# A new instruction order for a linear-attention kernel with a gated scan behind it

## The chip, the cores and the metric

The kernel runs on one core of one Trainium2 chip. The metric is the device time in microseconds (us). Times come from several executions, each with its own span (first to last instruction of the profile) and its own mean granted clock of TensorE. Below, a *hole* is a stretch in which TensorE stands idle, and a *fall* is a drop of its granted clock to half.

## The reference, cut to what matters

```python
# attention part; q, k, v: 8 batches, 8 heads, 576 tokens, 64 wide
q_s = np.exp(q - np.max(q, axis=-1, keepdims=True))
q_s = q_s / (np.sum(q_s, axis=-1, keepdims=True) + 1e-09)
...                                    # k_s: the same over the tokens (axis 2)
kv = np.einsum('bhsd,bhse->bhde', k_s, v)
return np.einsum('bhsd,bhde->bhse', q_s, kv).astype(np.float32)

# gated scan part; x: the heads put side by side, 576 x 512 per batch
proj = x @ w_in
val, gate = (proj[..., :D_inner].copy(), proj[..., D_inner:].copy())
a = np.exp(A_log)[None, None, :]
...
for t in range(S):
    h = a[0, 0] * h + val[:, t, :]
    ys[:, t, :] = h
silu = gate * (1.0 / (1.0 + np.exp(-gate)))
return (silu * ys @ w_out).astype(np.float32)
```

(The first two lines join several of the original.)

## The kernel before: the parts that matter

The whole kernel is driven by one string, ORDER. Each entry emits the instructions of one step, and every engine executes its own instructions strictly in the order of this string. `norm/P.3.0` is the normalization of the first half of batch 3 on POOL (GpSimd); `/A` is ACT (ScalarE), `/D` is DVE (VectorE). Entries without a letter have a fixed engine. Tokens are cut in 9 chunks of 512 for the projections (`val`, `gate`), scans and outputs, and in 8 batches of 576 for the attention part.

```python
def decay(self, e, m):                       # one row of scan factors; e is the engine of the fill
    copy(e, decay[:, m], acol[:, m:m + 1].broadcast_to([128, 2 * W]))
    nc.gpsimd.memset(decay[:, m, W:W + 1], 0.0)     # the column where a batch begins: always GpSimd

def norm(self, e, b, q2):                    # eq *= 1 / row sum
    ...
def transp(self, e, b, g):                   # six 128 x 128 transposes of eq on TensorE
    ...
def kv(self, e, b, q2):                      # k^T v, 36 matmuls of 64 x 65
    ...
def xa(self, e, b, q2):                      # x^T, columns 0..503 of the batch
def xr(self, e, b):                          # x^T, the remaining 72 columns
def _proj(self, dst, i, col):                # four matmuls of 128 x 512 (val or gate)
    ...
RINGS = {..., "qf": 2, "kf": 2, "vf": 2, "tp": 1, "ax": 1, "pp": 3, "po": 2, ...}   # buffers
```

The detail on which this case turns is the second line of `decay`: an entry `decay/A.2` puts a long copy (1.04 us) into ACT's order and a tiny clearing (0.10 us) into GpSimd's order. The clearing has to wait for the copy.

The softmax here doesn't subtract the row's maximum and nothing guards it: scores larger than these inputs give would overflow.

## Time and profile before

| what | kernel before |
|---|---|
| time, median of 3 | 145.68 us |
| span of the profiled execution | 142.5 us (time 144.23 us), clock 1.000 |
| TensorE, VectorE, ScalarE, GpSimd busy | 119.6, 114.6, 98.9, 92.2 us |
| first projection starts | 22.89 us |
| first projection of chunk 1 starts | 37.99 us |
| last matmul ends | 138.46 us |

The lines of the profile are shown in the prediction below. Until about 38 us loads, softmax and casts set the pace; from there TensorE is practically never idle (busy 99.58 of the 100.47 us up to its last matmul). A time line entry reads: start, duration (both us), engine, source line, operation, output <- inputs, shapes, count, and in brackets how long the engine stood idle just before and whose end released it. The letter x with a number is the count of merged instructions.

```profile
26.63 0.10 POOL L232 MEMSET decay<- 128x1 f32 x1 [2.33 <-ACT decay L192]
26.75 2.12 POOL L263 TENSOR_TENSOR eq<-eq,qs 128x1152 bf16<-128x1152 bf16 x1
```

Here GpSimd stands 2.33 us at a clearing of one column, with the normalization of batch 2 behind it.

### The profile page before, as it was taken

What the parts mean: (1) busy time and instruction counts of PE and PEld (TensorE: products, weight loads), DVE (VectorE), ACT (ScalarE), POOL (GpSimd) and SP (SyncE); (2) the same over time, 40 slices, a digit from 0 to 9 for tenths busy, and PEclk for the clock granted to TensorE, in tenths of its full rate; (3) what the DMA queues carried; (4) which work ended last, traced back from release to release, by engine and by line L of the source; (5) the groups of instructions that cost most, each with busy time, mean ns of one, the idle gap of its engine ahead of it and who ended that gap; (6) DMA issues with size and microseconds to landing.
All of it is one profiled execution on the core that took longest, in us unless ns stands there. A gap on an engine that the chain in (4) does not pass through costs nothing.

```text
span 142.5 us, 3185 instructions
## 1 busy us (share of the span) xinstructions
PE 119.6 (84%) x1269; PEld 61.7 (43%) x1284; DVE 114.6 (80%) x146; ACT 98.9 (69%) x138; POOL 92.2 (65%) x80
## 2 busy tenths in 40 slices
PE   0024586987599999999999999999999999999980
...
DVE  0358669879998898989998889999789798989630
...
DMA  4999999999999999999999999999543433007195
GB/s 111 401 399 391 391 390 389 391 393 391 389 389 392 391 391 391 387 404 403 394 325 382 399 240 208 263 408 392 110 83 121 181 147 147 0 0 289 71 343 190
DMA packets 24243, 42.29 MB, mean 297 GB/s; under 512 B 5666, under 2 KB 5922, under 8 KB 24227
## 3 DMA queue, kind: packets, MB, share of 16 engines
...
HBM read 31.46 MB, written 9.44 MB: 287 GB/s over the span
## 4 chain that ended last, share of the span: by engine, by line
PE 70%; DMA 14%; DVE 5%; POOL 3%; issue 3%; SPq 2%; ACT 0%; POOLq 0%; ACTq 0%; DVEq 0%
PE pp L377 38%; PE po L423 21%; DMA kf<-in_k_dram 7%; DMA y<-in_moe_w_in_dram 6%; PE ax L290 4%; PE tp L271 3%; POOL eq L263 3%; SPq L188 2%; DVE qs L255 2%; PE pp L333 1%; PE ax L333 1%; DVE u L404 1%; DVE xT L194 1%; PE pp L423 1%; PE pp L360 1%
## 5 line engine op out<-in xcount | busy, mean ns | idle before, releaser
L377 PE MATMUL pp<-xT,win 128*128 128x512 bf16 (+1 forms) x308 | 68.0, 363 | 1.9 <-ACT xT L192 1.2
L408 POOL TENSOR_TENSOR z<-u,y 128x512 bf16<-128x512 f32 x29 | 37.3, 1297 | 24.2 <-DVE u L404 15.6
L377 PEld LDWEIGHTS <-win 128*128 128x128 bf16 x320 | 30.6, 99 | 31.5 <-issue 4.4
L396 DVE TENSOR_TENSOR_SCAN y<-decay,y,pp 128x512 f32<-128x512 f32 x32 | 39.6, 1262 | 1.4 <-PE pp L377 1.3
L263 POOL TENSOR_TENSOR eq<-eq,qs 128x1152 bf16<-128x1152 bf16 x16 | 33.8, 2119 | 7.9 <-DVE qs L258 7.7
L423 PE MATMUL po<-wout,z 128*128 128x512 bf16 x134 | 33.7, 379 | 0.3
L401 ACT ACTIVATE th<-pp 128x512 f32<-128x512 f32 x36 | 21.5, 597 | 15.8 <-PE pp L377 15.6
L404 DVE SCALAR_TENSOR_TENSOR u<-th,pp 128x512 f32<-128x512 f32 x36 | 24.4, 683 | 5.3 <-ACT th L401 4.8
L255 DVE TENSOR_REDUCE qs<-eq 128x36 f32<-128x2304 bf16 (+1 forms) x10 | 20.6, 2057 | 6.6 <-ACT eq L235 6.6
L271 PE MATMUL tp<-ident,eq 128*128 128x128 bf16 x108 | 10.9, 249 | 13.3 <-POOL eq L263 11.8
L235 ACT ACTIVATE eq<-qf 128x1152 bf16<-128x1152 f32 x16 | 18.3, 1158 | 5.3 <-DMA qf<-in_q_dram 5.3
L430 ACT ACTIVATE ob<-po 128x512 f32<-128x512 f32 x28 | 16.6, 599 | 7.6 <-PE po L423 7.6
L423 PEld LDWEIGHTS <-z 128*128 128x128 bf16 x148 | 13.9, 98 | 15.3 <-issue 1.0
L241 ACT ACTIVATE ek<-kf 128x2304 bf16<-128x2304 f32 (+1 forms) x10 | 17.2, 1736 | 0.5 <-DMA kf<-in_k_dram 0.5
L194 POOL CAST vb<-vf 128x1152 bf16<-128x1152 f32 (+1 forms) x14 | 14.9, 1080 | 3.7 <-DMA vf<-in_v_dram 3.6
L271 PEld LDWEIGHTS <-eq 128*128 128x128 bf16 x108 | 8.3, 111 | 17.4 <-POOL eq L263 13.2
L192 ACT ACTIVATE xT<-pp 128x504 bf16<-128x504 f32 (+1 forms) x20 | 7.8, 443 | 4.4 <-PE pp L333 2.6
L290 PE MATMUL ax<-vb,ek 64*64 64x65 bf16 x576 | 7.3, 199 | 1.5 <-ACT ek L241 1.1
L290 PEld LDWEIGHTS <-ek 64*64 64x64 bf16 x576 | 6.2, 112 | 4.7 <-issue 2.2
L192 ACT ACTIVATE eqT<-tp 128x768 bf16<-128x768 bf16 x8 | 6.5, 810 | 1.6 <-PE tp L271 1.6
L192 ACT ACTIVATE xT<-ax 128x1008 bf16<-128x1008 f32 x7 | 7.1, 1016 | 0.3 <-PE pp L360 0.3
L432 DVE TENSOR_SCALAR ob<-po 128x512 f32<-128x512 f32 x6 | 4.1, 684 | 3.2 <-PE po L423 3.2
...
## 6 DMA issues: line engine op xcount, KB each, us to landing
...
```

The lines of the kernel that those rows point to most:

```text
L192: nc.scalar.activation(out, in_, AF.Copy)
L235: nc.scalar.activation(buf("eq", b)[:, q2].rearrange("p c h d -> p h c d"), buf("qf", b)[:, 2 * q2:2 * q2 + 2].rearrange("p h (c d) -> p h ...
L255: nc.vector.tensor_reduce(s[:, 0, n].rearrange("p (a o) -> p a o", o=1), buf("eq", b)[:, h].rearrange("p q c h d -> p (q c h) d"), axis=AX ...
L263: eng[e].tensor_tensor(x, x, r.rearrange("p (a o) -> p a o", o=1) .broadcast_to([128, 2 * C, D]), ALU.mult)
L271: nc.tensor.transpose(tp[:, j, :], src[:, 6 * g + j, :], ident)
L290: nc.tensor.matmul(kvp[o:o + 64, h2, q2 * E1:(q2 + 1) * E1], lhsT=ek[r, 2 * q2 + hp2, c * D:(c + 1) * D], rhs=vb[r, 2 * q2 + hp2, c, :], s ...
L377: nc.tensor.matmul(dst[:, a:z], lhsT=win[:, kt, col:col + 128], rhs=xT[:, kt, s0:s0 + z - a], start=(kt == 0), stop=(kt == 3))
L396: nc.vector.tensor_tensor_scan(buf("y", (i, m)), a, buf("pp", ("v", i, m)), init, op0=ALU.mult, op1=ALU.add)
L401: nc.scalar.activation(buf("th", (i, m)), buf("pp", ("g", i, m)), AF.Tanh, scale=0.5)
L404: nc.vector.scalar_tensor_tensor(buf("u", (i, m)), buf("th", (i, m)), 1.0, buf("pp", ("g", i, m)), op0=ALU.add, op1=ALU.mult)
L408: eng[e].tensor_tensor(buf("z", i)[:, m], buf("u", (i, m)), buf("y", (i, m)), ALU.mult)
L423: nc.tensor.matmul(self._po(i, r, h), lhsT=buf("z", i)[:, m, r * 128:(r + 1) * 128], rhs=wout[:, m, self._cols(h)], start=(m == 0), stop=( ...
```

## The change

The intent: a new order of instructions and loads for all engines, in which TensorE finds work earlier. The two strings hold the same 556 entries; some of them change engine. The load of A_log goes from SP's queue to ACT's. New forms of the transposes and of the projections are added as methods, but no entry of the new order uses them. Cut to its core:

```diff
-lq.0.1 expq.0.1 lq.0.0 lq.1.- qsum.0.1 expq.0.0 norm/P.0.1 qsum.0.0 transp.0.2 expq.1.0 lk.0.0
-...
-val.1.0 vcast/P.2.0 tanh.1.2 gmul.1.2 vcast/P.2.1 val.1.3 expk.2.- norm/P.3.0 gate.1.1 scan.1.0
-transp.3.0 val.1.2 tanh.1.1 tevac/A.3.0 scan.1.3 norm/P.3.1 kv.2.0 cwout/A.0 gmul.1.1 scan.1.2
-...
+lalog lq.0.1 lq.0.0 lq.1.- expq.0.1 qsum.0.1 lk.0.1 lv.0.0 expq.0.0 norm/P.0.1 expq.1.0 expk.0.1
+...
+xbevac/D.1.1 cwout/A.1 tevac/A.2.2 gate.1.2 gate.1.0 qsum.3.- tanh.1.2 tanh.1.0 expk.2.-
+zmul/P.0.2 decay/P.0 val.1.0 outp.0.3 decay/A.2 gmul.1.2 outp.0.2 gmul.1.0 lq.4.- oevac/A.0.3
+oevac/A.0.2 norm/P.3.0 val.1.2 scan.1.0 transp.3.0 vcast/P.2.1 gate.1.3 gate.1.1 tanh.1.3 lk.3.-
+...
-            nc.sync.dma_start(out=alog, in_=moe_A_log.rearrange("(o n) -> o n", o=1))
+            nc.scalar.dma_start(out=alog, in_=moe_A_log.rearrange("(o n) -> o n", o=1))
+        def transp4(self, e, b, g):        # not called by the new order
+        ...
-        def _proj(self, dst, i, col):
+        def _proj(self, dst, i, col, q2=None):      # q2 is always None in the new order
```

The scan factors are filled in another order and on other engines, too: before `decay/A.3 decay/P.2 decay/A.0 decay/P.1`, now `decay/A.1 decay/P.3 decay/P.0 decay/A.2`.

More of the change, by code (lines that the diff above doesn't have):

```diff
@@ L23 @@
 ORDER = """
-lq.0.1 expq.0.1 lq.0.0 lq.1.- qsum.0.1 expq.0.0 norm/P.0.1 qsum.0.0 transp.0.2 expq.1.0 lk.0.0
-tevac/A.0.2 lv.0.1 norm/P.0.0 transp.0.0 lk.0.1 expk.0.0 expq.1.1 qsum.1.0 tevac/D.0.0
-vcast1/P.0.2 lalog lv.0.0 expk.0.1 norm/P.1.0 vcast1/D.0.3 vcast1/P.0.0 qsum.1.1 vcast1/A.0.1
-transp.0.1 tevac/D.0.1 lq.2.- kv.0.1 lwin.0.0 lwin.2.0 lwin.3.0 kv.0.0 transp.1.0 tevac/A.1.0
-lwin.1.0 lwin.1.1 norm/P.1.1 kvn.0 lwin.0.1 xt.0.0.1 xt.0.1.1 cwin/P.2.0 expq.2.0 xevac/D.0.0.1
-transp.1.1 xt.0.0.0 tevac/D.1.1 xevac/A.0.1.1 transp.1.2 xt.0.1.0 xevac/D.0.0.0 lwin.2.1
@@ L30 @@
-cwin/D.0.0 cwin/P.1.0 cwin/P.3.0 lwin.3.1 cwin/P.1.1 xevac/D.0.1.0 expq.2.1 talog val.0.3 acol
-tevac/A.1.2 lk.1.- cwin/A.2.1 cwin/P.0.1 val.0.1 lv.1.- cwin/A.3.1 gate.0.0 decay/A.3 qsum.2.-
-scan.0.3 gate.0.3 tanh.0.0 scan.0.1 norm/P.2.0 decay/P.2 gmul.0.0 norm/P.2.1 tanh.0.3 vcast/P.1.1
-gmul.0.3 expk.1.1 transp.2.0 val.0.0 expk.1.0 lq.3.- scan.0.0 gate.0.2 val.0.2 tanh.0.2
-tevac/D.2.0 vcast/A.1.0 gate.0.1 zmul/P.0.3 transp.2.1 kv.1.1 gmul.0.2 scan.0.2 kv.1.0 lv.2.-
-tanh.0.1 lk.2.- lwout.0 kvn.1 lwout.1 gmul.0.1 lq.4.- xr.1 xrevac/D.1 xa.1.0 decay/A.0
@@ L36 @@
-tevac/D.2.1 expq.3.0 expq.3.1 lk.3.- xa.1.1 xbevac/A.1.1 zmul/P.0.0 xaevac/A.1.0 transp.2.2
-tevac/A.2.2 xbevac/D.1.0 gate.1.3 tanh.1.3 zmul/P.0.1 zmul/P.0.2 gate.1.2 qsum.3.- gmul.1.3
-val.1.0 vcast/P.2.0 tanh.1.2 gmul.1.2 vcast/P.2.1 val.1.3 expk.2.- norm/P.3.0 gate.1.1 scan.1.0
-transp.3.0 val.1.2 tanh.1.1 tevac/A.3.0 scan.1.3 norm/P.3.1 kv.2.0 cwout/A.0 gmul.1.1 scan.1.2
-gate.1.0 tanh.1.0 kv.2.1 expq.4.0 transp.3.1 cwout/P.1 kvn.2 expq.4.1 outp.0.2 tevac/D.3.1 xr.2
-decay/P.1 xa.2.0 transp.3.2 zmul/P.1.2 xrevac/D.2 gmul.1.0 outp.0.3 lv.3.- xa.2.1 qsum.4.-
@@ L42 @@
-val.1.1 lq.5.- zmul/P.1.0 zmul/P.1.3 oevac/A.0.2 xaevac/A.2.0 lv.4.- lk.5.- oevac/A.0.3
-vcast/P.3.1 xbevac/A.2.0 vcast/P.3.0 xbevac/A.2.1 scan.1.1 tevac/D.3.2 outp.0.0 outp.0.1 expk.3.-
-val.2.2 gate.2.1 scan.2.2 tanh.2.1 oevac/A.0.0 val.2.1 lk.4.- gmul.2.1 kv.3.1 kv.3.0 gate.2.0
-oevac/A.0.1 gate.2.2 expq.5.1 tanh.2.0 store.0.1 norm/P.4.0 zmul/P.1.1 scan.2.1 kvn.3 gmul.2.0
-tanh.2.2 val.2.3 transp.4.0 expq.5.0 norm/P.4.1 gmul.2.2 scan.2.3 outp.1.0 xa.3.0 xr.3 outp.1.1
-zmul/P.2.2 tevac/A.4.0 xrevac/A.3 lq.6.- qsum.5.- oevac/A.1.0 xa.3.1 xbevac/A.3.0 lv.5.-
@@ L48 @@
-xbevac/A.3.1 vcast/P.4.0 vcast/P.4.1 zmul/P.2.1 gate.2.3 outp.1.3 transp.4.1 tanh.2.3 val.2.0
-tevac/D.4.1 norm/P.5.1 gmul.2.3 scan.2.0 xaevac/A.3.0 zmul/P.2.3 transp.4.2 oevac/A.1.1 val.3.1
-val.3.3 expk.4.- scan.3.1 scan.3.3 tevac/D.4.2 norm/P.5.0 expk.5.- oevac/A.1.3 val.3.0 kv.4.1
-kv.4.0 gate.3.0 tanh.3.0 zmul/P.2.0 scan.3.0 outp.1.2 val.3.2 vcast/P.5.0 gate.3.2 gmul.3.0
-vcast/P.5.1 expq.6.0 oevac/A.1.2 tanh.3.2 expq.6.1 scan.3.2 kvn.4 transp.5.0 gate.3.1 outp.2.3
-gmul.3.2 tevac/D.5.0 xa.4.0 store.0.0 zmul/P.3.2 store.1.0 xr.4 zmul/P.3.0 tanh.3.1 xaevac/A.4.0
@@ L54 @@
-outp.2.0 gmul.3.1 xrevac/A.4 transp.5.1 oevac/A.2.3 kv.5.1 kv.5.0 store.1.1 lk.6.- xa.4.1
-gate.3.3 xbevac/A.4.1 qsum.6.- kvn.5 xbevac/A.4.0 outp.2.2 val.4.1 tanh.3.3 tevac/A.5.1
-oevac/A.2.0 gate.4.2 zmul/P.3.1 norm/P.6.0 gmul.3.3 tanh.4.2 transp.5.2 val.4.2 scan.4.1 gmul.4.2
-zmul/P.3.3 gate.4.0 tevac/A.5.2 gate.4.1 oevac/A.2.2 tanh.4.0 outp.3.1 scan.4.2 lv.6.- lq.7.-
-gmul.4.0 dtransp.6.0 vcast/P.6.0 xa.5.0 xa.5.1 tanh.4.1 gmul.4.1 store.2.1 oevac/D.3.1
-xbevac/D.5.1 norm/P.6.1 vcast/P.6.1 outp.2.1 expk.6.- val.4.0 xaevac/A.5.0 xbevac/D.5.0 outp.3.0
@@ L60 @@
-scan.4.0 kv.6.0 xr.5 zmul/P.4.2 dtransp.6.1 kv.6.1 val.4.3 xrevac/A.5 gate.5.1 zmul/D.4.1
-expq.7.1 gate.4.3 oevac/D.2.1 oevac/A.3.0 scan.4.3 zmul/P.4.0 tanh.5.1 tanh.4.3 kvn.6 expq.7.0
-outp.3.2 val.5.1 lv.7.- gmul.5.1 gmul.4.3 val.5.2 outp.3.3 scan.5.1 zmul/P.4.3 oevac/A.3.2 xa.6.1
-scan.5.2 zmul/P.5.1 outp.4.2 xbevac/A.6.0 store.2.0 store.3.0 qsum.7.- xbevac/A.6.1 xr.6
-vcast/P.7.0 oevac/A.3.3 xa.6.0 val.5.0 xrevac/A.6 outp.4.0 vcast/A.7.1 norm/P.7.1 val.5.3
-scan.5.0 oevac/A.4.2 xaevac/A.6.0 gate.5.3 scan.5.3 lk.7.- store.3.1 tanh.5.3 gate.5.2 tanh.5.2
@@ L66 @@
-outp.4.3 gmul.5.3 gate.6.0 gate.5.0 oevac/D.4.0 gmul.5.2 tanh.6.0 gmul.6.0 zmul/P.5.3 tanh.5.0
-val.6.2 gmul.5.0 val.6.3 outp.4.1 expk.7.- scan.6.2 gate.6.2 kv.7.1 kv.7.0 gate.6.3 oevac/A.4.1
-tanh.6.2 scan.6.3 dtransp.7.1 norm/P.7.0 gmul.6.2 kvn.7 zmul/D.5.2 val.6.1 dtransp.7.0 tanh.6.3
-oevac/A.4.3 zmul/P.5.0 val.6.0 gmul.6.3 outp.5.3 scan.6.1 scan.6.0 outp.5.2 zmul/D.6.2
-oevac/A.5.3 xr.7 xa.7.0 store.4.1 outp.5.1 xrevac/A.7 store.4.0 xa.7.1 xaevac/A.7.0 xbevac/D.7.0
-gate.6.1 xbevac/A.7.1 oevac/D.5.2 gate.7.0 val.7.0 zmul/P.6.0 tanh.6.1 tanh.7.0 gmul.6.1 gmul.7.0
@@ L72 @@
-outp.5.0 val.7.2 oevac/D.5.1 zmul/P.6.3 gate.7.2 scan.7.0 zmul/P.6.1 scan.7.2 outp.6.3 store.5.1
-val.7.3 oevac/A.5.0 gate.7.1 tanh.7.2 gmul.7.2 scan.7.3 tanh.7.1 gmul.7.1 gate.7.3 tanh.7.3
-val.8.2 val.7.1 gmul.7.3 zmul/P.7.0 val.8.0 outp.6.1 oevac/A.6.3 outp.6.0 scan.8.2 gate.8.1
-scan.7.1 scan.8.0 gate.8.2 zmul/D.7.3 oevac/A.6.1 tanh.8.1 gmul.8.1 gate.8.0 zmul/D.7.2
-zmul/D.7.1 oevac/A.6.0 tanh.8.2 outp.6.2 gmul.8.2 tanh.8.0 store.5.0 val.8.1 outp.7.2 val.8.3
-gmul.8.0 store.6.0 scan.8.1 oevac/A.6.2 oevac/A.7.2 zmul/P.8.2 gate.8.3 outp.7.3 tanh.8.3
@@ L78 @@
-scan.8.3 store.6.1 zmul/P.8.1 gmul.8.3 zmul/D.8.3 outp.7.1 oevac/A.7.3 outp.7.0 oevac/A.7.1
-zmul/P.8.0 store.7.1 oevac/A.7.0 outp.8.0 store.7.0 oevac/A.8.0 outp.8.1 store.8.0 outp.8.2
-outp.8.3.1 oevac/A.8.1 oevac/A.8.3.1 outp.8.3.0 store.8.1 oevac/D.8.2 store.8.3.1 store.8.2
-oevac/D.8.3.0 store.8.3.0
+lalog lq.0.1 lq.0.0 lq.1.- expq.0.1 qsum.0.1 lk.0.1 lv.0.0 expq.0.0 norm/P.0.1 expq.1.0 expk.0.1
+qsum.0.0 lk.0.0 lv.0.1 transp.0.2 norm/P.0.0 lq.2.- tevac/D.0.2 transp.0.0 qsum.1.0 expq.1.1
+expk.0.0 tevac/D.0.0 transp.0.1 vcast1/P.0.1 norm/P.1.0 lwin.1.1 tevac/D.0.1 qsum.1.1
@@ new lines @@
+vcast1/D.0.3 transp.1.0 lwin.2.1 lwin.0.0 vcast1/P.0.0 lwin.3.1 vcast1/P.0.2 tevac/A.1.0 kv.0.0
+norm/P.1.1 kv.0.1 kvn.0 lwin.0.1 expq.2.0 xt.0.0.1 lwin.2.0 xevac/D.0.0.1 xt.0.0.0 xt.0.1.0
+expq.2.1 cwin/P.1.1 transp.1.1 tevac/A.1.1 xt.0.1.1 xevac/D.0.1.0 talog cwin/A.0.1 xevac/D.0.1.1
+acol cwin/P.0.0 lwin.1.0 lwin.3.0 xevac/D.0.0.0 cwin/P.2.1 cwin/D.3.1 transp.1.2 lk.1.- gate.0.0
+lv.1.- lq.3.- gate.0.1 cwin/P.2.0 decay/A.1 gate.0.3 qsum.2.- lwout.0 tanh.0.0 tanh.0.1
+norm/P.2.0 cwin/D.3.0 gmul.0.0 cwin/A.1.0 tanh.0.3 lwout.1 gmul.0.1 gmul.0.3 tevac/D.1.2
@@ new lines @@
+norm/P.2.1 val.0.3 val.0.1 scan.0.3 expk.1.1 transp.2.0 tevac/A.2.0 scan.0.1 expk.1.0 val.0.0
+scan.0.0 val.0.2 transp.2.1 vcast/A.1.1 tevac/A.2.1 gate.0.2 zmul/P.0.3 vcast/P.1.0 kv.1.0 kv.1.1
+scan.0.2 tanh.0.2 zmul/P.0.1 decay/P.3 kvn.1 xa.1.0 gmul.0.2 xr.1 transp.2.2 xrevac/D.1
+zmul/P.0.0 cwout/P.0 xaevac/D.1.0 expq.3.0 xa.1.1 expq.3.1 lk.2.- xbevac/A.1.0 lv.2.-
+xbevac/D.1.1 cwout/A.1 tevac/A.2.2 gate.1.2 gate.1.0 qsum.3.- tanh.1.2 tanh.1.0 expk.2.-
+zmul/P.0.2 decay/P.0 val.1.0 outp.0.3 decay/A.2 gmul.1.2 outp.0.2 gmul.1.0 lq.4.- oevac/A.0.3
@@ new lines @@
+oevac/A.0.2 norm/P.3.0 val.1.2 scan.1.0 transp.3.0 vcast/P.2.1 gate.1.3 gate.1.1 tanh.1.3 lk.3.-
+tanh.1.1 scan.1.2 tevac/D.3.0 vcast/P.2.0 expq.4.1 kv.2.1 expq.4.0 kv.2.0 gmul.1.3 kvn.2 gmul.1.1
+val.1.3 outp.0.0 xr.2 xa.2.0 norm/P.3.1 outp.0.1 lv.3.- xrevac/A.2 scan.1.3 xaevac/A.2.0 xa.2.1
+transp.3.1 val.1.1 lk.4.- xbevac/A.2.1 xbevac/A.2.0 qsum.4.- val.2.2 zmul/P.1.0 scan.1.1
+tevac/A.3.1 transp.3.2 gate.2.2 zmul/P.1.3 zmul/P.1.2 scan.2.2 expk.3.- gate.2.1 vcast/P.3.0
+tanh.2.2 vcast/P.3.1 norm/P.4.0 kv.3.0 kv.3.1 val.2.1 tevac/D.3.2 tanh.2.1 gmul.2.2 gate.2.3
@@ new lines @@
+gmul.2.1 expk.4.- scan.2.1 zmul/P.1.1 tanh.2.3 gate.2.0 transp.4.0 oevac/A.0.0 val.2.3
+oevac/A.0.1 kvn.3 outp.1.3 gmul.2.3 tevac/D.4.0 lq.5.- lv.4.- outp.1.2 val.2.0 scan.2.3 tanh.2.0
+zmul/P.2.1 xa.3.0 gmul.2.0 store.0.1 expq.5.0 expq.5.1 lk.5.- xr.3 oevac/D.1.3 xaevac/A.3.0
+norm/P.4.1 xrevac/A.3 vcast/P.4.0 scan.2.0 transp.4.1 oevac/A.1.2 outp.1.0 vcast/P.4.1 kv.4.0
+xa.3.1 kv.4.1 xbevac/A.3.1 tevac/D.4.1 qsum.5.- zmul/P.2.0 zmul/P.2.3 store.0.0 xbevac/A.3.0
+lq.6.- transp.4.2 zmul/P.2.2 outp.1.1 oevac/A.1.0 norm/P.5.0 lv.5.- val.3.2 expk.5.- gate.3.2
@@ new lines @@
+gate.3.0 kvn.4 tanh.3.2 outp.2.3 scan.3.2 val.3.0 oevac/A.1.1 tanh.3.0 gmul.3.2 val.3.1
+tevac/D.4.2 gmul.3.0 transp.5.0 scan.3.0 zmul/P.3.2 norm/P.5.1 oevac/A.2.3 vcast/P.5.0 outp.2.2
+xa.4.0 expq.6.1 vcast/P.5.1 expq.6.0 xr.4 xrevac/A.4 outp.2.0 scan.3.1 tevac/D.5.0 xaevac/A.4.0
+xa.4.1 gate.3.1 qsum.6.- xbevac/A.4.0 transp.5.1 oevac/D.2.2 xbevac/A.4.1 lv.6.- lk.6.- store.1.1
+gate.3.3 tanh.3.1 val.3.3 tevac/A.5.1 kv.5.0 kv.5.1 norm/P.6.0 tanh.3.3 gmul.3.1 expk.6.-
+zmul/P.3.0 gmul.3.3 outp.2.1 val.4.0 lq.7.- store.1.0 gate.4.1 scan.3.3 zmul/P.3.1 zmul/P.3.3
@@ new lines @@
+gate.4.0 oevac/A.2.0 tanh.4.1 scan.4.0 gmul.4.1 transp.5.2 gate.4.3 val.4.1 tanh.4.0 oevac/A.2.1
+vcast/P.6.0 outp.3.0 tanh.4.3 gmul.4.0 kvn.5 oevac/A.3.0 gmul.4.3 scan.4.1 norm/P.6.1 zmul/P.4.0
+tevac/A.5.2 val.4.3 store.2.1 dtransp.6.0 expq.7.0 val.4.2 outp.3.1 scan.4.3 xa.5.0 oevac/A.3.1
+xa.5.1 outp.3.2 dtransp.6.1 store.2.0 scan.4.2 vcast/P.6.1 xbevac/D.5.1 gate.4.2 xaevac/A.5.0
+xbevac/A.5.0 kv.6.0 kv.6.1 oevac/D.3.2 xr.5 tanh.4.2 outp.3.3 zmul/D.4.3 xrevac/A.5 gmul.4.2
+kvn.6 expq.7.1 zmul/D.4.2 val.5.2 gate.5.2 scan.5.2 zmul/P.4.1 oevac/A.3.3 outp.4.3 tanh.5.2
@@ new lines @@
+gmul.5.2 xa.6.1 outp.4.2 qsum.7.- xbevac/A.6.0 xbevac/A.6.1 xr.6 xa.6.0 lv.7.- gate.5.3 lk.7.-
+store.3.1 norm/P.7.1 xrevac/A.6 gate.5.1 gate.5.0 tanh.5.3 tanh.5.1 gmul.5.3 gmul.5.1 tanh.5.0
+oevac/A.4.3 oevac/A.4.2 gmul.5.0 vcast/P.7.1 xaevac/A.6.0 vcast/A.7.0 val.5.0 expk.7.- scan.5.0
+val.5.3 val.5.1 zmul/P.5.2 norm/P.7.0 scan.5.3 scan.5.1 outp.4.0 outp.4.1 val.6.0 scan.6.0
+gate.6.1 zmul/P.5.1 tanh.6.1 val.6.2 zmul/P.5.0 store.3.0 dtransp.7.1 gmul.6.1 kv.7.0 kv.7.1
+gate.6.3 tanh.6.3 oevac/A.4.0 gate.6.2 scan.6.2 gate.6.0 zmul/D.5.3 oevac/A.4.1 tanh.6.0 gmul.6.3
@@ new lines @@
+kvn.7 dtransp.7.0 tanh.6.2 gmul.6.0 outp.5.3 oevac/A.5.3 zmul/P.6.0 val.6.1 gmul.6.2 outp.5.2
+scan.6.1 xr.7 xa.7.0 xrevac/A.7 outp.5.0 xa.7.1 xaevac/A.7.0 zmul/P.6.1 val.6.3 xbevac/A.7.1
+xbevac/D.7.0 gate.7.0 store.4.0 zmul/P.6.2 oevac/A.5.2 tanh.7.0 scan.6.3 val.7.1 gate.7.2
+gmul.7.0 zmul/P.6.3 outp.5.1 val.7.0 tanh.7.2 store.4.1 scan.7.1 gate.8.2 gmul.7.2 oevac/A.5.1
+oevac/A.5.0 tanh.8.2 scan.7.0 gmul.8.2 val.7.2 gate.7.1 store.5.1 tanh.7.1 scan.7.2 gate.8.0
+outp.6.3 zmul/P.7.0 gmul.7.1 tanh.8.0 gmul.8.0 oevac/D.6.3 val.8.2 zmul/P.7.2 outp.6.2 val.7.3
@@ new lines @@
+scan.8.2 scan.7.3 oevac/A.6.2 gate.7.3 tanh.7.3 gmul.7.3 zmul/D.8.2 outp.6.0 store.6.1
+oevac/A.6.0 store.5.0 val.8.0 val.8.1 outp.6.1 zmul/P.7.3 scan.8.0 scan.8.1 val.8.3 gate.8.1
+zmul/D.7.1 gate.8.3 oevac/A.6.1 tanh.8.1 outp.7.3 tanh.8.3 oevac/A.7.3 scan.8.3 gmul.8.3 gmul.8.1
+outp.7.2 zmul/P.8.0 outp.7.0 oevac/A.7.2 outp.7.1 store.6.0 zmul/P.8.3 oevac/A.7.0 zmul/D.8.1
+outp.8.1 store.7.1 outp.8.0 oevac/A.7.1 store.7.0 oevac/A.8.1 oevac/D.8.0 store.8.1 store.8.0
+outp.8.3.1 outp.8.2 outp.8.3.0 oevac/A.8.2 oevac/A.8.3.0 oevac/D.8.3.1 store.8.3.1 store.8.2
@@ L82 @@
+store.8.3.0
 """
```

25 lines of the change are left out of this document (17 added, 8 removed).

## The prediction

> **What bounds the kernel now.** I read the busy rows of the page first, then the chain that ended last in order of time, then the order of time of TensorE for the first 48 us, and last the waits of VectorE. The page:
>
> ```profile
> PE 119.6 (84%) x1269; PEld 61.7 (43%) x1284; DVE 114.6 (80%) x146; ACT 98.9 (69%) x138; POOL 92.2 (65%) x80
> ...
> PE   0024586987599999999999999999999999999980
> ...
> DVE  0358669879998898989998889999789798989630
> ...
> DMA  4999999999999999999999999999543433007195
> ...
> GB/s 111 401 399 391 391 390 389 391 393 391 389 389 392 391 391 391 387 404 403 394 325 382 399 240 208 263 408 392 110 83 121 181 147 147 0 0 289 71 343 190
> ```
>
> A slice is 142.5/40 = 3.56 us. TensorE has nothing in slices 1 and 2, is half filled in slices 3 to 11 (to about 38 us), and from there stands at 9 almost to the end. So there are two stages: an opening of some 38 us in which loads, sums and casts decide when TensorE can work, and 100 us in which TensorE is the bound. The queue moves about 390 GB/s from the second slice on, but in the second stage that is prefetch. The chain says the same:
>
> ```profile
> 14.53 9.10 DMA y<-in_moe_w_in_dram
> ...
> 26.75 2.13 POOL eq L263
> ...
> 36.80 2.47 DVE qs L255
> ...
> 137.58 0.89 PE pp L423 x8
> ...
> 138.49 0.42 DVE ob L432
> ```
>
> The first links are loads (k, v, then w_in), then softmax work of GpSimd and VectorE, and from 42.6 us practically only TensorE. The next view is TensorE in order of time; in brackets stands its idle time and what ended it:
>
> ```profile
> 16.50 0.71 PE L290 MATMUL ax<-vb,ek 64*64 64x65 bf16 x36 [0.41 <-POOL vb L194]
> ...
> 22.37 0.58 PE L225 MATMUL ax<-one,alog 1*128 1x1 f32 x4 [0.87 <-DVE xT L194]
> 22.89 0.61 PE L377 MATMUL pp<-xT,win 128*128 128x512 bf16 x1
> 23.71 4.55 PE L377 MATMUL pp<-xT,win 128*128 128x512 bf16 x14 [0.22 <-POOL win L194]
> 28.92 0.51 PE L271 MATMUL tp<-ident,eq 128*128 128x128 bf16 x6 [0.66 <-POOL eq L263]
> 29.27 3.62 PE L377 MATMUL pp<-xT,win 128*128 128x512 bf16 x16
> ...
> 34.78 0.26 PE L360 MATMUL pp<-eqT,kvc 64*64 64x72 bf16 x8 [0.76 <-DVE kvc L300]
> ...
> 37.99 4.48 PE L377 MATMUL pp<-xT,win 128*128 128x512 bf16 x19 [1.23 <-ACT xT L192]
> ```
>
> The first projection starts at 22.89, all eight of chunk 0 are through at about 32.7, and chunk 1 starts at 37.99. Sixteen matmuls take 3.45 us in the chain at 29.43, so 0.216 us each and 0.863 us for a chunk-column of four. One number decides what an order can give: the big groups of four are 72 projections and 36 outputs, 108 x 0.863 = 93.2 us. With 7 x 0.71 us of the kv products, 15 x 0.34 us of transposes (batches 1 to 5, three each), 14 x about 0.21 us and 7 x about 0.1 us of x^T products, that is some 107 us, and TensorE ends at 138.47. Everything else, 31 us, is the opening and its holes; the order can win only there.
>
> **What the Trainium skill says.** "TensorE: Matmul & The Clock Gate", Part 1, says that an idle array runs at half clock and is released by about 3.4 us of sustained work, in a free-running window. The trace agrees: the weight loads of the first projections start 0.43 us apart (24.57, 25.00, 25.42), those after 29 us belong to matmuls of 0.216 us; the change falls near 26.6 us, 3.7 us after the first projection. The page's PEclk row is 9 throughout and does not show it. "DMA: Bandwidth & Descriptors", section "Issuing engines are not separate DMA queues", says that transfers of all issuing engines run on the same 16 engines and another issuer saves only issue time. That bears on the A_log load, moved from SP to ACT; its issue takes 0.37 us at 4.04 in the trace. "Perfetto Trace Analysis", section "Identifying the Most-Contended Engine", warns that matmul busy time is no measure of the distance to the roofline; here a projection matmul is listed with 363 ns and comes every 216 ns, so I use the spacing.
>
> **The change, part by part.** The two orders hold the same 556 operations; only places and engines differ. The new transpose forms and the halved projections are defined but no entry of the new order calls them, so the 128-wide transposes as such cost and save 0. "No longer wait for the remainder columns" is likewise only an order: in both kernels chunk i reads up to token 512(i+1), and batch i's main columns reach 576i+504, which covers it. In the opening, the remainder product of batch 1 takes 0.26 us, so its removal ahead of chunk 1 is worth at most that plus its evacuation, 0.52 us.
>
> Engine moves on VectorE: one more w_in cast (+0.42), one more x^T evacuation of batch 0 (+0.76), the 1008-wide one of batch 1 (+1.2, twice the 0.67 of a 504-wide one less a little), against one 504-wide (-0.67), one remainder (-0.52), one output (-0.68) and one z product (-0.66): about 0. So the sum of no engine changes; timing does.
>
> Opening, worked through in order from the durations of the trace. Batch 0's four k/v halves still land at about 11.2, 12.7, 14.2 and 15.8 us, but in the new order: the last is now the v half of heads 4 to 7. It is cast in two halves; one sits on VectorE behind a q sum of 1.34 + 0.27 us that begins about 14.9. So this cast ends at 16.5 + 0.75 = 17.25 us, kv ends at about 17.95 (0.71), where before it ended at 17.2: about +0.8 us. The four x^T evacuations follow on VectorE almost back to back, 19.2 to 22.4 us; before, one was on ACT and the last ended at 22.3. So this loss is nearly made good.
>
> Then w_in. Before, the four pieces of the val half come first; the first projection needs only these. Landings follow from casts that wait for them: second 20.17, fourth 21.50, fifth 23.00, sixth 23.68, seventh 24.32. Afterwards gate comes first and its four pieces are the first, second, fourth and fifth. The fifth holds the first rows, which the first matmul needs: 23.00 + 0.63 us of cast on ACT = 23.65. So the first projection starts 0.75 us later than 22.89, and the clock is released later too, at some 27 us.
>
> Gate 0.0, 0.1, 0.3 then run to about 28 us (two at 1.71 us cold, one warm), the first val column waits for a cast that ACT makes between two tanh (28.4), and VectorE becomes the link: gate product to 29.65, transpose copy to 30.2, four scans of 1.2 us to 35.0, kv normalization 0.6, gate product 0.65, remainder copy 0.5, the 1008-wide evacuation 1.2 and a 504-wide 0.65 = 38.65 us. Chunk 1 starts at about 38.7 instead of 37.99, with exactly the same matmul work done: **+0.7 us**.
>
> Afterwards: VectorE still has the q sum of batch 3 before it (2.54 + 0.38), which before began at 36.72; but two output groups (2 x 0.86 us) are placed there, which need no new VectorE result. At the start of chunk 2 there is less between the x^T products and the first projection (two outputs are gone from there), and its evacuations are in ACT's order behind two exponentials of 1.15 us; I find a hole of about 0.6 us near 51 us. The other ends of waits come in time. Sum +0.7 + 0.6 = +1.3 us if nothing elsewhere is won. Of the rest I credit -0.6 us: in several batches both kv halves or x^T products now stand together, and before shows some 1.4 us over the pure sum between 38 and 59.4 us, in part at such switches. The last chunk has four outputs of chunk 7 (3.45 us) between the last gate and the first output of chunk 8, while the last z product needs about 2.8 us: no hole, and the tail after TensorE, 142.5 - 138.5 = 4.0 us, stays. Net +0.7 us, held with little confidence as to sign.
>
> **The rivals.** First: the opening is shorter, not longer. VectorE's four evacuations and the scans placed together leave fewer interlocks, GpSimd no longer stands 2.3 us at the decay fill before normalizing batch 2, and k comes earlier in the later loads. Holes before 38 us are about 0.66 + 0.76 + 1.23 plus 1.9 us of half clock; taking most of them gives -2 us, 143.5 us. Against it speaks that w_in's fifth piece and the scans bound the opening in my working. Second: the half clock lasts a window longer, since the first dense stretch starts 0.75 us later in a free-running window: eight more matmuls at 0.43, +1.7 us, of which VectorE's chain hides about 1; 147 us or a little more. Third: the order of the second stage makes waits for VectorE, at 90% there. Its work after the q sum of batch 3 comes to about 88 us out of 97, so it has 9 us; a wait now and then costs 1 to 2 us, 147.5 us. Fourth: loads become the bound. Against: reads are 31.46 MB, at 0.39 MB/us 81 us, and the order of k and v from batch 2 on moves landings by 3 us at most where use lies further off.
>
> **Range and chances.** 145.68 + 0.7 = 146.4 us; as a new order by someone who tunes is more often a gain than my hand working sees, I take 146.1. Opening errors of 1 us either way, clock window 0 to 1.7 us, holes 1 us either way: 143.8 to 148.4 us. Faster by over 2% means under 142.8 and needs nearly all holes of the opening gone: 0.07. Slower by over 2% means over 148.6: 0.08. The rest, 0.85, within 2%.
>
> **What would show it.** Right: the first projection at about 23.7 us with ACT's w_in cast as releaser, chunk 1 at 38 to 39.5 us with an x^T evacuation of VectorE as releaser, TensorE at 9 from slice 11 on, and the same 4 us after its last matmul. Wrong on the opening if chunk 1 starts before 37 us; wrong on the second stage if the time from chunk 1's start to the last matmul, 100.5 us before, changes by more than 1 us.

## The result, and the profile after

| | before | after |
|---|---|---|
| time, median of 4 | 145.69 us (145.24 to 145.88) | 147.82 us (147.42 to 148.42) |
| ratio | | 1.0154 (95%: 1.0108 to 1.0200) |
| span of the profiled execution | 142.5 us, clock 1.000 | 145.6 us, clock 0.981 |
| chunk 1 starts | 37.99 us | 37.05 us |
| last matmul ends | 138.46 us | 141.27 us |

A ratio here is the mean time of one kernel's fast runs over that of the kernel before's fast runs of the same rounds, so it is not quite the ratio of the medians beside it. The change made the kernel slower by 1.5%, clear of noise, though within 2%.

The busy rows of the changed kernel, 40 slices of 3.64 us each:

```profile
PE   0024678996865999999999999999999999999970
...
DVE  0357779599993599999999799899988698899730
...
POOL 3087962969929979999996999006981843334300
PEclk9999999999996999999999999999999999999997
```

The kernel before had a full TensorE row from slice 12 on, 39 us. Now the row has an 8, a 6 and a 5 in slices 11 to 13, VectorE has a 3 in slice 13, GpSimd a 2 in slice 12, and the granted clock is 6 tenths in slice 13. After that TensorE's row is as full as before (the 7 in the last slice of the clock lies behind the last matmul). So one place, 40 to 48 us, stands out. All engines in order of time there:

```profile
39.80 2.12 ACT L241 ACTIVATE ek<-kf 128x2304 bf16<-128x2304 f32 x1 [0.21 <-DMA kf<-in_k_dram]
40.08 0.10 POOL L232 MEMSET decay<- 128x1 f32 x1
...
41.83 1.04 ACT L192 ACTIVATE decay<-acol 128x1024 f32<-128x1024 f32 x1
...
42.92 0.10 POOL L232 MEMSET decay<- 128x1 f32 x1 [2.75 <-ACT decay L192]
43.02 2.12 POOL L263 TENSOR_TENSOR eq<-eq,qs 128x1152 bf16<-128x1152 bf16 x1
...
45.19 0.82 PE L271 MATMUL tp<-ident,eq 128*128 128x128 bf16 x6 [2.79 <-POOL eq L263]
...
45.80 2.98 PE L394 MATMUL pp<-xT,win 128*128 128x512 bf16 x8
```

Read it downward as a chain. ACT is in the exponential of k until 41.92 us and only then fills decay row 2. GpSimd has been ready since 40.18 us, but the next instruction in its order is the clearing of a column in that row, so it stands 2.75 us for 0.10 us of work. Behind the clearing stands the normalization of batch 3, whose own input (the row sums) was complete at 40.46 us. TensorE in turn stands 2.79 us at the transposes of batch 3, with two gate columns behind them whose inputs are there (a run below lets them go first). In the kernel before, the same normalization starts at 40.43 us, straight after GpSimd's casts, and TensorE has no hole at these transposes:

```profile
40.43 4.19 POOL L263 TENSOR_TENSOR eq<-eq,qs 128x1152 bf16<-128x1152 bf16 x2
...
42.61 0.51 PE L271 MATMUL tp<-ident,eq 128*128 128x128 bf16 x6
```

The second loss is in the last line. Eight projection matmuls take from 45.80 to 48.71 us; four of them at full clock take 0.863 us. The windows view of the changed kernel (columns: stretch, its length, busy us and count of TensorE, its weight loads, VectorE, ACT, GpSimd, then the granted clock, the DMA share and GB/s) shows it:

```profile
42.40:45.20 2.80, 0.01 (x2) 0.01 (x1) 1.66 (x2) 1.44 (x3) 2.28 (x3) 0.89 1.05 391
45.20:48.70 3.50, 3.50 (x14) 1.59 (x14) 0.87 (x2) 0.60 (x1) 3.50 (x3) 0.60 1.06 392
48.70:138.00 89.30, 88.51 (x950) 45.20 (x963) 80.46 (x97) 65.09 (x100) 60.04 (x44) 1.00 0.73 249
```

The clock is at 0.60 of full on average in the 3.5 us after the hole; cut finer, it falls at about 44.6 us, 2.2 us into the hole, and is full again at about 48.0 us. From 48.70 to 138 us TensorE is busy 88.51 us of 89.30; the kernel before has 88.72 us in the same stretch. The account of the two profiled executions: chunk 1 starts 0.94 us earlier; from there to the end of the last matmul 104.22 us instead of 100.47, so 3.75 us more, of which the hole is 2.79 us and the slow matmuls about 1.0 us (eight matmuls at the chain's 2.77 us instead of 1.73). The slow transposes add some 0.3 us (0.61 us until the next matmul instead of 0.34), so that about 0.35 us must have been won elsewhere. The tail after the last matmul is 0.3 us longer. 3.75 - 0.94 + 0.3 = 3.1 us, the difference of the spans.

The medians differ by 2.1 us, not by 3.1, because the profiled execution of the kernel before is one of its quick ones: it was at clock 1.000 and 144.23 us, while executions of the same kernel in later rounds at 0.985 to 0.988 took mostly 145.1 to 146.3 us (three at 0.988 took 144.2). The mean clock is a rough guide only, since it also counts falls behind the last matmul, which slow no matmul: one in the changed kernel's profile begins at about 143.6 us and makes some 0.007 of the 0.019 that its clock is short of 1.

### The profile page after: what moved, and what is told of

Read it like the earlier page. It is cut to its first block, busy times and chain, and to the rows that moved or that the text cites. A ratio compares the mean times of both kernels' runs of the same rounds, so it can differ in the third digit from the quotient of the medians.

```text
span 145.6 us, 3183 instructions
## 1 busy us (share of the span) xinstructions
PE 120.7 (83%) x1268; PEld 62.3 (43%) x1284; DVE 114.8 (79%) x144; ACT 98.0 (67%) x139; POOL 93.0 (64%) x81
## 4 chain that ended last, share of the span: by engine, by line
PE 70%; DMA 13%; POOL 8%; issue 3%; SPq 1%; ACT 1%; DVE 1%; ACTq 0%; DVEq 0%; POOLq 0%
PE pp L394 41%; PE po L436 19%; DMA vf<-in_v_dram 7%; DMA y<-in_moe_w_in_dram 6%; POOL z L425 3%; PE ax L306 3%; PE tp L271 3%; POOL eq L263 1%; POOL decay L194 1%; SPq L188 1%; PE pp L349 1%; PE ax L349 1%; DVE y L413 1%; POOL vb L194 1%; PE pp L436 1%
## 5 line engine op out<-in xcount | busy, mean ns | idle before, releaser
L394 PE MATMUL pp<-xT,win 128*128 128x512 bf16 (+1 forms) x311 | 70.2, 370 | 1.8 <-DVE xT L194 0.9
L425 POOL TENSOR_TENSOR z<-u,y 128x512 bf16<-128x512 f32 x30 | 38.3, 1285 | 19.7 <-DVE u L421 11.1
L394 PEld LDWEIGHTS <-win 128*128 128x128 bf16 x320 | 31.3, 101 | 33.0 <-issue 5.1
L413 DVE TENSOR_TENSOR_SCAN y<-decay,y,pp 128x512 f32<-128x512 f32 x32 | 40.1, 1269 | 2.7 <-PE pp L394 2.1
L194 POOL CAST vb<-vf 128x1152 bf16<-128x1152 f32 (+1 forms) x15 | 15.5, 1053 | 0.8 <-DMA vf<-in_v_dram 0.8
L192 ACT ACTIVATE xT<-pp 128x144 bf16<-128x144 f32 (+1 forms) x23 | 8.9, 432 | 3.2 <-PE pp L376 2.0
L194 DVE COPY eqT<-tp 128x768 bf16<-128x768 bf16 x10 | 5.5, 548 | 4.3 <-PE tp L271 4.3
L192 ACT ACTIVATE xT<-ax 128x1008 bf16<-128x1008 f32 x6 | 6.1, 1016 | 0.8 <-PE pp L376 0.8
```

The lines of the kernel that those rows point to most:

```text
L192: nc.scalar.activation(out, in_, AF.Copy)
L194: eng[e].tensor_copy(out, in_)
L394: nc.tensor.matmul(dst[:, a:z], lhsT=win[:, kt, col:col + 128], rhs=xT[:, kt, s0:s0 + z - a], start=(kt == 0), stop=(kt == 3))
L413: nc.vector.tensor_tensor_scan(buf("y", (i, m)), a, buf("pp", ("v", i, m)), init, op0=ALU.mult, op1=ALU.add)
L425: eng[e].tensor_tensor(buf("z", i)[:, m], buf("u", (i, m)), buf("y", (i, m)), ALU.mult)
```

## The experiments

The theory: GpSimd's blocked clearing makes the normalization late, TensorE stands 2.8 us, and its clock falls for a while. Rivals: the second stage is worse in many places through the new places of loads and outputs; the load of A_log and the order of w_in pieces; the clock alone. All kernels gave correct results. The runs below are fast unless said otherwise.

### The clearing moved ahead, in the changed kernel

```diff
-... tanh.1.0 expk.2.- zmul/P.0.2 decay/P.0 val.1.0 outp.0.3 decay/A.2 gmul.1.2 ...
+... tanh.1.0 decay/A.2 expk.2.- zmul/P.0.2 decay/P.0 val.1.0 outp.0.3 gmul.1.2 ...
```

> The changed kernel with one entry moved: ACT's fill of the third decay row stands before the exponential of k of batch 2, not after it. Theory (GpSimd waits 2.75 us for that fill to clear one column, so the normalization of batch 3 is late, TensorE stands 2.8 us before its transposes and its clock drops for one window): both the wait and the drop go, 2.8 + 1.5 = about 4 us less than the changed kernel, so 143.5 to 144.5 us, faster than the kernel before by 1 us. Rival (the second stage is worse in many places, through the new places of outputs and loads): at most 1.5 us less, still slower than the kernel before.

Measured: 146.70 us (146.04 to 147.43), ratio 1.0091 (1.0027 to 1.0155). This was a miss: 1.1 us less than the changed kernel and still slower than the kernel before is what the rival had named. But the fault lay in the edit. The entry carries both halves, so the clearing moved forward in GpSimd's order as well, ahead of a z product:

```profile
41.74 0.10 POOL L230 MEMSET decay<- 128x1 f32 x1 [2.78 <-ACT decay L190]
41.80 1.27 POOL L423 TENSOR_TENSOR z<-u,y 128x512 bf16<-128x512 f32 x1
...
43.13 1.47 PE L434 MATMUL po<-wout,z 128*128 128x512 bf16 x6 [1.73 <-POOL z L423]
...
46.38 0.51 PE L269 MATMUL tp<-ident,eq 128*128 128x128 bf16 x6 [0.92 <-POOL eq L261]
```

GpSimd stands just as long (2.78 us), only at another place, and TensorE now stands 1.73 us for z and 0.92 us for the transposes. The clock stayed up in this profile (0.997). So the run decides neither for the theory nor for the rival; it shows that this edit moved the wait and did not take it away.

### The same blockade put into the kernel before

```diff
-... val.1.3 expk.2.- norm/P.3.0 gate.1.1 scan.1.0 ...          (decay/A.0 25 entries earlier)
+... val.1.3 expk.2.- decay/A.0 norm/P.3.0 gate.1.1 scan.1.0 ...
```

> The kernel before with one entry moved the wrong way: ACT's fill of decay row 0 now stands after the exponential of k of batch 2 and before the normalization of batch 3. Theory: GpSimd waits some 3 us at the clearing of the column, TensorE stands some 3 us before the transposes of batch 3, and the clock may drop: 3 to 4.5 us slower, 148.5 to 150 us. Rival (this wait is covered by other work): less than 1 us.

Measured: 148.79 us (148.65 to 148.93), ratio 1.0234 (1.0185 to 1.0282). The profile, all engines in order of time:

```profile
43.35 0.10 POOL L230 MEMSET decay<- 128x1 f32 x1 [3.01 <-ACT decay L190]
...
45.62 0.51 PE L269 MATMUL tp<-ident,eq 128*128 128x128 bf16 x6 [3.33 <-POOL eq L261]
```

One entry at the wrong place costs the kernel before 3.3 us (148.79 against 145.52 of the same rounds), a fall of the clock behind the hole included (half from about 46.2 to 49.6 us). The blockade is enough by itself to make a loss of this size; nothing else of the change is in this run.

### The clearing done by ACT, in the changed kernel

Here every entry stays in its place. Only the clearing after an ACT fill is done by ACT:

```diff
-            nc.gpsimd.memset(decay[:, m, W:W + 1], 0.0)
+            if e == "ACT":
+                nc.scalar.activation(decay[:, m, W:W + 1], acol[:, m:m + 1], AF.Copy, scale=0.0)
+            else:
+                nc.gpsimd.memset(decay[:, m, W:W + 1], 0.0)
```

> The changed kernel with every entry in its place; only the clearing of the one column after an ACT fill is done by ACT itself, so that nothing of it stands in GpSimd's order. Theory (the blocked clearing delays the normalization of batch 3): GpSimd starts it right after the q sum, at about 40.5 us, the transposes follow without the 2.8 us hole; 2 to 3.5 us less than the changed kernel, 144.3 to 145.8 us, so level with the kernel before or up to 1% faster. Rival (GpSimd or TensorE would then stand at the next input, as in the run with the fill moved ahead): 147 us.

Measured: 144.93 us (144.23 to 145.66, 6 runs), ratio 1.0009 (0.9951 to 1.0067). The changed kernel's whole loss is gone:

```profile
40.61 2.12 POOL L264 TENSOR_TENSOR eq<-eq,qs 128x1152 bf16<-128x1152 bf16 x1 [0.46 <-DVE qs L259]
...
42.78 0.51 PE L272 MATMUL tp<-ident,eq 128*128 128x128 bf16 x6 [0.40 <-POOL eq L264]
...
43.12 1.89 PE L395 MATMUL pp<-xT,win 128*128 128x512 bf16 x8
```

The normalization starts at 40.61 us, as expected, and is now released by VectorE's row sums. TensorE stands 0.40 us in place of 2.79, and the eight projections behind the transposes take 1.89 us in place of 2.98. The clock of five of six runs was 0.992 or more; in the four executions of the changed kernel it was 0.975 to 0.986. In the profile of this run (0.992) the one fall begins at about 140.5 us, behind the last matmul at 138.4. This settles the cause of the loss. It also says what the rest of the change is worth: with the blockade gone it is level with the kernel before, within 0.7% either way.

### The clearing done by ACT, in the kernel before

The same edit in the kernel before, where GpSimd stood 2.33 us at 26.63 us.

> The kernel before with the same clearing on ACT. There GpSimd stood 2.3 us for the third row at 26.6 us, before the normalization of batch 2, and TensorE 0.66 us for the transposes after it. Theory (a wait costs what TensorE stands in the end): at most 0.7 us less, more likely 0 to 0.5, since VectorE's chain sets the start of chunk 1. Rival (each us that GpSimd stands is paid): 2 us less.

Measured: ratio of the fast runs 0.9981 (0.9875 to 1.0086); of six runs three were fast (143.72, 145.41 and 145.54 us). The normalization of batch 2 starts at 25.11 us in place of 26.75, and the first projection of chunk 1 starts at 38.14 us, where it was at 37.99:

```profile
25.11 2.12 POOL L264 TENSOR_TENSOR eq<-eq,qs 128x1152 bf16<-128x1152 bf16 x1 [0.35 <-ACT win L190]
...
38.14 0.58 PE L378 MATMUL pp<-xT,win 128*128 128x512 bf16 x1 [1.84 <-ACT xT L190]
```

So in this profile 1.6 us won on GpSimd did not bring chunk 1 forward: the same kind of wait that costs 3.3 us at 43 us brings no delay at 26 us, where the last x^T evacuation, not GpSimd, sets when TensorE goes on. The times alone, with 1% of room either way, would not show it.

### TensorE's order changed instead

The transposes of batch 3 go behind two gate columns, so that TensorE has work while GpSimd stands:

```diff
-... scan.1.0 transp.3.0 vcast/P.2.1 gate.1.3 gate.1.1 tanh.1.3 ... tevac/D.3.0 ... gmul.1.3 ...
+... scan.1.0 vcast/P.2.1 gate.1.3 gate.1.1 transp.3.0 tanh.1.3 ... gmul.1.3 tevac/D.3.0 ...
```

> The changed kernel with the transposes of batch 3 moved behind two gate columns of chunk 1 in TensorE's order (their copy on VectorE with them); the clearing of the decay column and GpSimd's wait stay. Theory (GpSimd's lateness costs through TensorE's strict order only): about 1.7 us of gate work goes into the hole, the clock stays up; 2 to 3 us less than the changed kernel, with some of the hole turning up before the kv product of batch 2, whose cast on GpSimd is late too. Rival (TensorE would have stood there for other inputs): under 1 us.

Measured: 147.28 us (146.60 to 147.38), ratio 1.0135 (1.0046 to 1.0224), little better than the changed kernel. A miss in size:

```profile
45.15 0.51 PE L269 MATMUL tp<-ident,eq 128*128 128x128 bf16 x6 [0.74 <-POOL eq L261]
46.24 0.48 PE L304 MATMUL ax<-vb,ek 64*64 64x65 bf16 x36 [0.58 <-POOL vb L192]
...
47.33 0.72 PE L304 MATMUL ax<-vb,ek 64*64 64x65 bf16 x36 [0.61 <-POOL vb L192]
```

The hole is broken in three, 0.74 + 0.58 + 0.61 = 1.93 us in place of 2.79, and the clock, which was to stay up, fell all the same (half from about 47.3 to 50.8 us). The casts of v for the kv product stand in GpSimd's order behind the same late normalization. Here the late engine was met again by its next reader.

### The openings and second stages exchanged

First the changed order up to chunk 1 and then the order of the kernel before for what is left; then the other way round.

> The changed kernel's order up to the first projection of chunk 1, then the order of the kernel before for all that is left. Theory: opening 0.9 us shorter and the second stage of the kernel before (100.5 us to the last matmul): about 144.7 us. Rival (the gain of the opening is given back because work is only shifted): 145.7 us.

Measured: 150.32 us (150.26 to 150.49), ratio 1.0356 (1.0268 to 1.0444). A clear miss: the seam made a worse hole at the same transposes, this time behind a load. In the new opening the loads of w_out come ahead of k and v of batch 2, and in the old second stage GpSimd's cast of that v stands ahead of the normalization of batch 3:

```profile
42.88 2.24 POOL L192 CAST vb<-vf 128x1152 bf16<-128x1152 f32 x2 [1.91 <-DMA vf<-in_v_dram]
45.07 4.19 POOL L261 TENSOR_TENSOR eq<-eq,qs 128x1152 bf16<-128x1152 bf16 x2
...
47.25 0.82 PE L269 MATMUL tp<-ident,eq 128*128 128x128 bf16 x6 [4.27 <-POOL eq L261]
```

The new opening itself was intact (chunk 1 at 37.09 us). This order of the second stage was good only with the loads it was made for.

> The order of the kernel before up to the first projection of chunk 1, then the changed kernel's order for what is left. The third decay row is by then filled, so the blocked clearing is not there. Theory: with the block gone the changed second stage is as good as the one before within 1 us: 145 to 146.5 us. Rival (the changed second stage is worse in itself): 147 us or more.

Measured: 147.74 us (146.91 to 148.46), ratio 1.0193 (1.0077 to 1.0310). The hole at the transposes of batch 3 is not there, and in the profiled execution (146.91 us) the second stage is as long as before once the clock is taken out: 102.19 us from chunk 1 to the last matmul, with its first twelve matmuls at 4.44 us where they take 2.76 at full clock, so 100.5 us. But two executions took 148.3 to 148.5 us, and for them there is no profile. A mixed order also has its own seam (GpSimd stood 3.8 us for another decay fill at 40.21 us, and TensorE 0.40 us for w_out). By its time alone the run lies where the rival had put it (147 us or more). What it would say of the changed second stage stays open; the run with the clearing on ACT says it better.

### The place of the A_log load

> The kernel before with the load of A_log alone moved to ACT's queue and to the front. Theory ([...]one load less lets the fifth w_in piece be issued 1.5 us earlier and land about 1 us earlier): the fifth piece lands at about 22.0 instead of 23.0 us. In this order the first projections need only the first four pieces, so the first projection stays at about 22.9 us and the time changes by less than 0.7 us. Rival (only the order of pieces and evacuations matters): landings unchanged.

Measured: 145.66 us (144.22 to 146.01), ratio 0.9997 (0.9915 to 1.0080). The time was as expected, the earlier landing was not: GpSimd's casts that wait for w_in pieces went on at 22.45 us in this profile and at 21.50 us in the kernel before.

> The changed kernel with the load of A_log put back on SP, third before the last load of batch 0, as in the kernel before. Theory: the fifth w_in piece, which the first gate column needs, lands about 1 us later, the first projection starts at 23.6 instead of 22.7 us, chunk 1 at 37.5 to 38 instead of 37.05 us; 0.3 to 1 us slower than the changed kernel. Rival (A_log's place does not matter): unchanged within 0.3 us.

Measured: 147.56 us, ratio of the fast runs 1.0064 (0.9989 to 1.0138). Two of four runs were fast, 146.18 and 146.45 us at clock 0.995 and 0.998; two were slow, 148.66 and 149.55 us at 0.982 and 0.974. The profile, a fast one, has the same hole at the transposes (2.46 us), but no fall of the clock behind it:

```profile
45.59 0.51 PE L269 MATMUL tp<-ident,eq 128*128 128x128 bf16 x6 [2.46 <-POOL eq L261]
```

The kernel before shows no effect of this load. In the changed kernel the two fast runs lie some 1.5 us below the runs with the load on ACT's queue, but the profiled one of them is without a fall and the slow two are not quicker, so nothing is shown there either. The cast of the fifth w_in piece, which waits for its load, began at 22.03 us in the first profile of the changed kernel and at 21.82 us with the clearing on ACT, but at 22.94 to 23.20 us in the seven other profiles with this opening (six with A_log on ACT's queue, one on SP's). This landing varies from run to run.

These runs help in another way: a hole of 2.5 us without a fall of the clock puts the kernel at 146.2 to 146.5 us, the kernel before without a fall is at 144.1 to 144.2 us in the same rounds. So the hole alone is some 2 us, an estimate from two runs, and the fall adds to that in the runs that have it.

### The clock

Two runs try to hold the clock with matmuls on zeros that nothing reads. The first puts twelve of them ahead of the transposes of batch 3 in the changed kernel, the blockade left in.

> The changed kernel with twelve matmuls on zeros into a spare PSUM slot ahead of the transposes of batch 3, so that TensorE is busy through its wait for GpSimd. The wait stays. Theory: the clock doesn't drop, the eight projections after the wait take 1.73 instead of 2.77 us and the transposes 0.34 instead of 0.8; 1.2 to 1.6 us less than the changed kernel, about 146.3 us. Rival (the half clock is only shown, or its loss is hidden behind VectorE): no change.

Measured: 147.79 us (147.28 to 148.13), ratio 1.0177 (1.0087 to 1.0267), no gain. Time line of TensorE:

```profile
37.68 4.45 PE L393 MATMUL pp<-xT,win 128*128 128x512 bf16 x12 [0.93 <-DVE xT L193]
...
44.56 2.75 PE L400 MATMUL pp<-zero 128*128 128x512 bf16 x12
47.15 0.50 PE L270 MATMUL tp<-ident,eq 128*128 128x128 bf16 x6
```

In this execution the clock fell earlier, at the start of chunk 1 (twelve matmuls in 4.45 us), and that moved ACT's fill and with it the hole further back. After the zeros the transposes ran at full speed (0.50 us against 0.82). So the run does not tell what the fall alone costs. It does show that the fall is not bound to that hole: chunk 1 comes after a sparse stretch. The kernel before has it too, in some executions, as the run with its A_log load moved happens to show:

```profile
38.01 6.06 PE L375 MATMUL pp<-xT,win 128*128 128x512 bf16 x20 [1.27 <-ACT xT L190]
```

Twenty matmuls take 6.06 us there, and 4.48 for nineteen in the first profile.

The second run has the clearing on ACT and seven matmuls on zeros in the two holes before chunk 1.

> As the first of these, with seven matmuls on zeros in TensorE's two short holes before chunk 1 (three after the kv product, four before the first gate column). Theory on the clock (a sparse stretch from 33 to 38 us lets the clock fall to half for a window in a part of the runs): the mean granted clock is 0.995 or above in all runs, and the time is at the fast end, 143.5 to 144.7 us, with little spread. Rival (the fall does not come from these holes, or zeros don't count): clocks of 0.988 and below as before, time as in the first of these.

Measured: 144.78 us (144.47 to 145.28, 6 runs), ratio 0.9997 (0.9944 to 1.0050). Clocks were 0.993 to 1.000 in all six, and the spread is 0.8 us; the fast runs of the kernel before in the same rounds went from 144.2 to 146.0 us. Without the zeros one run of six was at 0.988. That agrees with the sparse stretch as the trigger, but six runs do not settle it, all the less as the mean clock does not say where a fall lay; and the time is not better.

The last run adds eleven matmuls on zeros between 10 and 22 us.

> The run with the clearing on ACT and seven matmuls on zeros before chunk 1, and eleven more matmuls on zeros in TensorE's holes between 10.7 and 22.7 us, so that the clock may be released before the first gate column. Theory on the clock: the weight loads of the first gate columns are then 0.216 us apart instead of 0.43, the three columns end some 2 us earlier; VectorE's chain of gate products and scans starts earlier and chunk 1 begins 1 to 1.5 us earlier, so 143 to 144 us, faster than both kernels by about 1%. Rival (w_in casts and VectorE's chain hold chunk 1 where it is, or zeros do not release the clock): 144.4 to 145 us as without them.

Measured: 144.57 us (144.32 to 144.96), ratio 1.0010 (0.9965 to 1.0055). No gain:

```profile
19.13 0.51 PE L273 MATMUL tp<-ident,eq 128*128 128x128 bf16 x6
...
23.73 5.73 PE L396 MATMUL pp<-xT,win 128*128 128x512 bf16 x13 [1.84 <-ACT acol L227]
```

The clock was up by 19 us (six transposes in 0.51 us), so zeros do count. But TensorE then stood 1.84 us until the fifth w_in piece was cast (ACT's cast ended at 23.68 us; the profile names the short instruction right behind it), and the thirteen matmuls after it were slow again (5.73 us). No version tried here beats the kernel before.

Read together, these profiles say more of the fall. In eight of them (the changed kernel and seven runs) it comes between 37 and 48 us, and each time the clock is at half for 3.41 to 3.42 us; in the last run it is at half for 6.82 us from 22.89 us on. In the 3.41 us before each of the eight falls TensorE was busy 0 to 50% of the time. When these eight traces are cut in steps of 3.41 us forward and back from the fall, no step between 27 and 55 us with 55% or more was followed by one; the last run is an exception, with 59% before its fall. So what goes before a fall here is a stretch that is at most about half busy, whether one long hole makes it so or several short ones. Whether a hole of 2.5 to 2.8 us brings one may then depend on where such steps happen to lie; that is an inference, and no run tests it.

## Why the prediction was right or wrong

The time, 147.82 us, is inside the predicted range (143.8 to 148.4), and the class "within 2%" was given 0.85. The center was 146.1 us, 0.4 us above the kernel before; 2.1 us were measured. That the time fell inside was luck as far as the mechanism goes: of the two losses in its sum, the opening's 0.7 us had the wrong sign in most runs and the hole of 0.6 us is not there, while the hole that makes the loss is in none of its terms. By its own sign it was wrong on the second stage: from chunk 1 to the last matmul the time changed by 3.75 us, where more than 1 us was to count against it. Step by step:

- **The bound.** Right. From chunk 1 on TensorE is full before and after the one hole, and 48.7 to 138 us is the same in both kernels to 0.2 us.
- **The first projection 0.75 us later, at 23.65 us.** The profile of the changed kernel has 22.71 us, and the run with the clearing on ACT 22.50, but five of the runs that kept its opening (or changed A_log alone in it) have 23.62 to 23.88 us. The step was right for most runs, and so was the engine that releases it: the profile names ACT's exponential of A_log, which stands right behind the cast of the fifth piece, and that cast ended at 22.66 us.
- **Chunk 1 at 38.7 us, +0.7 us.** Wrong in sign in most runs: 37.03 to 37.68 us in five runs with this opening and 37.78 and 38.20 us in two, against 37.82 to 38.55 us in five with the one before. The releaser, a VectorE evacuation of x^T, was right. The sum was too large by 1.6 us in the first profile: the third gate product ended at 29.2 us and not at 29.65, the four scans took 4.54 us together and not 4.8, and the last term, a 504-wide evacuation of 0.65 us, is not on the path, since the first matmuls of chunk 1 read only what the 1008-wide one before it writes (it ended at 37.0 us).
- **A hole of about 0.6 us near 51 us.** Not there. TensorE goes on without a wait.
- **"The other ends of waits come in time."** This is the step that failed. The profile of the changed kernel shows TensorE standing 2.79 us before the transposes of batch 3, and the run with the clearing on ACT takes the whole loss back. I had named the same wait in the kernel before (GpSimd standing at the decay fill), and took its going as a gain for the change, but did not look for where the new order puts the entry that makes it.
- **The third rival,** waits in the second stage through the new order for 147.5 us, had the right size and the wrong engine: it was not VectorE at 90% (the trace of the kernel before has 86.8 us of 98.7 after that q sum, 88%) but GpSimd, which was idle for 2.75 us. The wait came from its order, not from its load.
- **The half clock.** Foreseen as a rival for the opening. There the half spacing of weight loads lasted to about 27.4 us (26.6 in the kernel before), not a whole window of 3.4 us longer. The fall that cost time came in the new hole, with about 1 us in the profiled execution.
- **Part by part.** That the unused transposes, the remainder columns and the engine moves are worth about nothing is consistent with the run at 1.0009, in which all of them are present.

## What to carry to other kernels

A tiny instruction on an engine with a strict order costs what stands behind it: before changing an order, list for each engine the entries that wait for another engine, and look at what follows them, above all where one entry of the program puts instructions on two engines. Consider letting the engine that writes a buffer also do the small fix-ups of it; here that took the whole loss back. And when an order is to be fixed, take the wait away; moving the waiter or the reader mostly moved the hole here.

## What the Trainium skill lacked or had wrong

- "TensorE: Matmul & The Clock Gate", Part 1 and its closing table, put the fall to half clock at an idle window of about 3.4 us and advise no gaps over about 3 us; the section on a second failure mode in the same part adds that frequent short gaps can do it, without a figure for how many. Here it fell at holes of 2.79 us (0.60 of full clock over the next 3.5 us), 1.84 us, and even where the longest single hole ahead was 0.93 us (the run with twelve zeros), in a sparse stretch of small matmuls. In the run with A_log back on SP a hole of 2.46 us went by without a fall. A share of busy time fits better: 0 to 50% in the 3.41 us before the eight falls between 37 and 48 us.
- The same page, Part 4, says of transposes that full clock "doesn't engage for transpose-mode". Here six transposes took 0.80 to 0.82 us before the clock was released or after it fell and 0.49 to 0.51 us at full clock, so they do run faster at full clock.
- No page that I found says that the record of the granted clock begins at full (the first page named warns only that these records can be unreliable): it gives 1.00 for 22.7 to 27.0 us of the kernel before, while the weight loads of its projections start 0.43 us apart, at half speed. Only later falls are in the record, so the mean clock of a run leaves the cold opening out. And it counts falls behind the last matmul: the 0.992 of the run with the clearing on ACT is one such fall, from about 140.5 us on.
